# Threshold attention and a two-layer MLP on one core: the shared tile on the whole array, the last stores by halves, a reordered first pair, and the half-swapped k by GpSimd instead of DMA

## The chip, the cores and the metric

The kernel runs on one core of one Trainium2 chip. The metric is the device time of one execution in microseconds (us). Engine names in the profile: PE is TensorE, PEld its weight loads, DVE is VectorE, ACT is ScalarE, POOL is GpSimd, SP is the sync engine, and "SPq" is the sync engine's DMA issues.

## The reference

```python
# q, k, v: (8, 8, 576, 64), tau = 0.02
scores = q @ k.T / sqrt(64)
scores = where(scores >= max(scores) - tau, scores, -1e9)
attn   = exp(scores - max(scores)); attn /= sum(attn) + 1e-9
x      = (attn @ v)                  # heads side by side: (4608, 512)
h      = x @ w_in                    # 512 -> 2048
out    = (h - tanh(h)) @ w_out       # 2048 -> 512, (4608, 512) float32
```

## The kernel before

Heads are handled in pairs, 32 pairs in all, four pairs to a batch. A head has 576 = 4 x 128 + 64 queries, so a pair has nine tiles of 128 queries: four of each head, and the **shared tile** (number 4), which holds the 64 leftover queries of both heads. Each of q and k is split into an fp16 high and an fp16 low half, and TensorE transposes both into kT and qT (low and high stacked over the partitions). The cross terms need kS, which is kT with its two halves of 64 partitions swapped. While a batch's attention runs, the MLP of the batch before is woven in. The MLP weights are loaded in 16 pieces during the first seven pairs and cast by GpSimd, which also splits q and k.

Four parts matter. First, the way kS is made:

```python
m = qk_pool.tile([P, W], FP16, name=f"{t}T", tag=t)
nc.vector.tensor_copy(out=m, in_=ps)
...
sw = qk_pool.tile([P, W], FP16, name="kS", tag="ks")
nc.sync.dma_start(out=sw[0:D, :], in_=m[D:P, :])
nc.sync.dma_start(out=sw[D:P, :], in_=m[0:D, :])
```

Second, the shared tile in `attend`, and its two transposes in `emit_x`:

```python
for c in range(5):                       # shared tile: ten narrow products
    n = 64 if c == 4 else P
    for hh in range(2):
        nc.tensor.matmul(
            out=po[64 * hh : 64 * hh + 64, 4, :],
            lhsT=pt[0:n, c * P + 64 * hh : c * P + 64 * hh + 64],
            rhs=vb[0:n, hh, c, :], start=(c == 0), stop=(c == 4))
...
for hh in range(2):                      # and two 64x64 transposes
    s = slice(64 * hh, 64 * hh + 64)
    nc.tensor.matmul(out=ps[s, 512:576], lhsT=o[s, 4, 0, :],
                     rhs=ident_bf[s, s], is_transpose=True, ...)
```

Third, the stores of the last MLP block (the leftover rows of all batches, 128 rows at a time):

```python
rows = out.rearrange("(b s) n -> b s n", b=B)
to = rows[2 * ms : 2 * ms + 2, MB:S, :]          # (2, 64, 512)
stores.append(lambda: nc.sync.dma_start(out=to, in_=yo))
```

Fourth, the first pair: an activation table is loaded first, then k, q and v are loaded whole, split whole, and turned whole, and only then do scores start.

Of the kernel before, what the change touches and what calls it, by code (L numbers as in the profile page):

```python
# [9 lines left out]
F32 = mybir.dt.float32  # L10
# [8 lines left out]
def kernel(  # L19
# [12 lines left out]
    P = 128  # L32
# [58 lines left out]
    for i in range(NM):  # L91
        zm = const.tile([P, 5 * P], BF16, name=f"zm{i}")
        nc.vector.memset(zm[:, S : 5 * P], -STEEP)
        zms.append(zm)

    pool = lambda name, bufs, **kw: ctx.enter_context(
        tc.tile_pool(name=name, bufs=bufs, **kw)
    )
# [18 lines left out]
    ps_y = pool("ps_y", 1, space=PSUM)  # L117

    ctx.enter_context(tc.manual_schedule())
    warm = const.tile([P, 1], F32, name="warm")  # L120
    nc.vector.memset(warm, 0.0)
    nc.scalar.activation(out=warm, in_=warm, func=ACT.Exp)


    raws = {}
# [3 lines left out]
    def load(p, t):  # L129
        b, h0 = p // HPAIR, 2 * (p % HPAIR)  # L130
        hs = slice(h0, h0 + 2)
        src = {"k": k, "q": q, "v": v}[t]
        eng = nc.scalar if p == 0 and t == "q" else nc.sync
        r = raws[p, t] = raw_pool.tile([P, 10, D], F32, name=f"{t}raw", tag=t)
        n = 8 if t == "v" else 10
        eng.dma_start(
            out=r[:, 0:n, :].rearrange("p (h c) d -> p h (c d)", h=2)[:, :, 0 : 4 * D],
            in_=src[b, hs, 0:512, :].rearrange("h (p c) d -> p h (c d)", c=4),
        )
        if t == "v":  # L140
            rem = src[b, hs, 512:S, :].rearrange("h s d -> s h d")
            eng.dma_start(out=r[0:64, 8:10, :], in_=rem)
            eng.dma_start(out=r[64:P, 8:10, :], in_=rem)
        else:
            eng.dma_start(out=r[:, 4, :], in_=src[b, hs, 512:S, :])

    hls = {}

    def split(p, t, fast=False):
        r = raws.pop((p, t))[:, 0:9, :]  # L150
        hl = hl_pool.tile([P, TPP, 2, D], FP16, name=f"{t}hl", tag=t)
        if fast:
            nc.scalar.mul(out=hl[:, :, 0, :], in_=r, mul=QKSC)
            nc.vector.scalar_tensor_tensor(
                out=hl[:, :, 1, :], in0=r, scalar=QKSC, in1=hl[:, :, 0, :],
                op0=ALU.mult, op1=ALU.subtract,
            )
        else:
            x = hl_pool.tile([P, TPP, D], F32, name="xs", tag="xs")
            nc.gpsimd.tensor_scalar(  # L160
                out=x, in0=r, scalar1=QKSC, scalar2=1.0, op0=ALU.mult, op1=ALU.mult
            )
            nc.gpsimd.tensor_copy(out=hl[:, :, 0, :], in_=x)
            nc.gpsimd.tensor_tensor(  # L164
                out=hl[:, :, 1, :], in0=x, in1=hl[:, :, 0, :], op=ALU.subtract
            )
        hls[p, t] = hl

    def split_v(p):
        r, vb = raws.pop((p, "v")), vbs[p % NV]  # L170
# [8 lines left out]

    mats = {}  # L180

    def turn(p, t):
        hl = hls.pop((p, t))
        ps = ps_big.tile([P, W], FP16, name=f"ps_{t}", tag="big")
        for c in range(TPP):
            nc.tensor.matmul(  # L186
                out=ps[:, c * P : (c + 1) * P],
                lhsT=hl[:, c, :, :].rearrange("p a d -> p (a d)"),
                rhs=ident_f16, is_transpose=True, start=True, stop=True,
            )  # L190
        m = qk_pool.tile([P, W], FP16, name=f"{t}T", tag=t)
        nc.vector.tensor_copy(out=m, in_=ps)  # L192
        mats[p, t] = m
        if t == "k" and p == 0:
            ps = ps_big.tile([P, W], FP16, name="ps_ks", tag="big")
            for c in range(TPP):
                for a in range(2):
                    nc.tensor.matmul(
                        out=ps[64 * a : 64 * a + 64, c * P : (c + 1) * P],
                        lhsT=hl[:, c, 1 - a, :],  # L200
                        rhs=ident_f16, is_transpose=True, start=True, stop=True,
                    )
            sw = qk_pool.tile([P, W], FP16, name="kS", tag="ks")
            nc.vector.tensor_copy(out=sw, in_=ps)
            mats[p, "ks"] = sw
        elif t == "k":
            sw = qk_pool.tile([P, W], FP16, name="kS", tag="ks")
            nc.sync.dma_start(out=sw[0:D, :], in_=m[D:P, :])
            nc.sync.dma_start(out=sw[D:P, :], in_=m[0:D, :])
            mats[p, "ks"] = sw  # L210


    MAIN = (slice(0, 512), slice(640, W))
# [101 lines left out]
    def attend(i):  # L315

        p, j = divmod(i, TPP)
        kd, vb = kind(j), vbs[p % NV]
        if kd == "A":
            return  # L320
        if j in (1, 6):
            ops[p, int(j > 4)] = ps_o.tile([P, 5, D + 1], F32, name="psO", tag="o")
        po = ops[p, int(j > 4)]
        if kd == "M":
            pt = pts.pop(i)
            for c in range(5):
                n = 64 if c == 4 else P
                for hh in range(2):
                    nc.tensor.matmul(  # L329
                        out=po[64 * hh : 64 * hh + 64, 4, :],  # L330
                        lhsT=pt[0:n, c * P + 64 * hh : c * P + 64 * hh + 64],
                        rhs=vb[0:n, hh, c, :], start=(c == 0), stop=(c == 4),
                    )
            return
        pt, hh = pts.pop(i), int(j > 4)

        for ab in range(2):
            blocks = [(4 * ab + ab + c, c) for c in range(4)]
            blocks.append((4, 4 + ab))
            for n, (blk, c) in enumerate(blocks):  # L340
                nc.tensor.matmul(  # L341
                    out=po[:, (j - 1 - 5 * hh) + ab, :],
                    lhsT=pt[:, blk * P : (blk + 1) * P], rhs=vb[:, hh, c, :],
                    start=(n == 0), stop=(n == 4),
                )
# [3 lines left out]
    def norm(p, hh):  # L349
        po = ops.pop((p, hh))  # L350
        if hh == 0:
            osb[p] = o_pool.tile([P, 5, 2, D], BF16, name="osb")
        n = 5 - hh
        rc = st_pool.tile([P, 5], F32, name="rc", tag="rc")
        nc.vector.reciprocal(out=rc[:, 0:n], in_=po[:, 0:n, D])
        nc.vector.tensor_tensor(
            out=osb[p][:, 0:n, hh, :], in0=po[:, 0:n, 0:D],
            in1=rc[:, 0:n].unsqueeze(2).to_broadcast([P, n, D]), op=ALU.mult,
        )

    xs = {}

    def emit_x(p):
        o = osb.pop(p)
        ps = ps_h.tile([P, S], BF16, name="psX", tag="h")
        for t in range(4):
            nc.tensor.matmul(
                out=ps[:, t * P : (t + 1) * P],
                lhsT=o[:, t, :, :].rearrange("p a d -> p (a d)"),
                rhs=ident_bf, is_transpose=True, start=True, stop=True,  # L370
            )
        for hh in range(2):
            s = slice(64 * hh, 64 * hh + 64)
            nc.tensor.matmul(
                out=ps[s, 512:576], lhsT=o[s, 4, 0, :], rhs=ident_bf[s, s],
                is_transpose=True, start=True, stop=True,
            )
        b = p // HPAIR
        if p % HPAIR == 0:
            xs[b] = x_pool.tile([P, DM_C, MB], BF16, name="xT")  # L380
        nc.vector.tensor_copy(out=xs[b][:, p % HPAIR, :], in_=ps[:, 0:512])
        nc.vector.tensor_copy(out=xR[:, p % HPAIR, b, :], in_=ps[:, 512:S])


    gs, stores = {}, []
# [29 lines left out]
    def project(m, ms, part, ps, last):  # L415
        for n in range(4 * part, 4 * part + 4):
            nc.tensor.matmul(  # L417
                out=ps, lhsT=gs[m][:, n, ms * P : (ms + 1) * P],
                rhs=w_out_sb[:, n, :], start=(n == 0), stop=(n == DF_C - 1),
            )  # L420
        if part == 3:
            yo = y_pool.tile([P, d_model], F32, name="yo")
            if last:
                nc.scalar.copy(out=yo, in_=ps)
            else:
                nc.vector.tensor_copy(out=yo, in_=ps)  # L426
            if m < B:
                rows = out[m * S : m * S + MB, :].rearrange("(p c) n -> c p n", c=4)
                to = rows[ms]
            else:  # L430
                rows = out.rearrange("(b s) n -> b s n", b=B)
                to = rows[2 * ms : 2 * ms + 2, MB:S, :]
            stores.append(lambda: nc.sync.dma_start(out=to, in_=yo))

    def layers(m, tail):

# [66 lines left out]
        for d, f in PREP[3 if p == 1 else 0 :]:  # L503
            plan.setdefault(first - d, []).append(lambda p=p, f=f: f(p))

    for t in ("k", "q", "v"):
        load(0, t)
    for t in ("k", "q"):
        split(0, t, fast=True)
    for t in ("k", "q"):  # L510
        turn(0, t)
    split_v(0)
    for t in ("k", "q", "v"):
        load(1, t)
# [8 lines left out]
    for s in range(-AHEAD, NTILE + LAG + 3):  # L523
# [7 lines left out]
            shift(s + AHEAD - 1)  # L531
        if 0 <= s + AHEAD < NTILE:
            scores(s + AHEAD)
        if 0 <= s + MASK < NTILE:
            kink(s + MASK)
        bend()
# [79 lines left out]
```

## Time and profile before

| | before |
|---|---|
| median of 3 runs | 579.23 us (577.52 to 580.37) |
| span of the profiled run | 576.3 us |
| first score product starts | 12.33 us |
| pairs 1 to 4 together | 50.3 us |
| five batches, pairs 8 to 27 | 60.5, 60.7, 62.7, 60.7, 60.5 us |
| last TensorE product ends / tail after it | 561.6 us / 14.6 us |

A pair or batch is counted from the start of its first score product to that of the next one's, read from the TensorE records. A wait table gives engine, line, what it waited for: us in total, times, longest. The page's views are shown in the prediction and two more behind it; a wait table gives engine, line, what it waited for: us in total, times, longest. The first is the wait table of the sync engine's DMA queue (engine, line, what it waited for: us in total, times, longest):

```profile
SPq L208 <- DVE nb L257: 64.9, 27, 9.3
```

L208 is the first kS issue. The releaser is inferred from VectorE's semaphore, and nb is the small instruction beside it; in the timeline the kT copy on VectorE ends at 30.67 us and this issue starts at 30.70. So the sync engine, which issues nearly every load, the transposes of z and the stores in order, stands still at this line for 65 us of the run, 24.5 of them between 14 and 75 us. The second is GpSimd's wait table for 20 to 75 us:

```profile
POOL w_in_sb L473 <- DMA wt<-in_moe_w_in_dram: 15.4, 4, 6.3
```

GpSimd waits there for the weight loads that stand in that queue.

### The profile page before, as it was taken

Reading aid. Unit: us, or ns where it says so; the run is one execution under the profiler, and the core shown is the slowest. Engines: PE = TensorE matmul, PEld = TensorE weight load, DVE = VectorE, ACT = ScalarE, POOL = GpSimd, SP = SyncE. Lnnn points to the kernel's source line nnn. Section 1 sums busy time; section 2 is a strip of 40 time slices with the busy share of each in tenths; the row PEclk is TensorE's granted clock in tenths of the full one; section 3 lists DMA queues with packets and bytes.
Section 4 is the critical chain, followed back from the end, with each engine's and each line's share of the span. In section 5 each row is a group of like instructions: output and inputs, shape, how many; then the busy total and the mean of one; then the engine's idle time right before and its main releaser. Section 6 shows DMA issues by size and latency. Waiting matters only on the chain.

```text
span 576.3 us, 13882 instructions
## 1 busy us (share of the span) xinstructions
PE 535.3 (93%) x5146; PEld 303.6 (53%) x5146; DVE 442.6 (77%) x1312; ACT 440.1 (76%) x634; POOL 215.6 (37%) x310
## 2 busy tenths in 40 slices
PE   3889899999999999998999999999999999999990
PEld 2566566665555555554555555555555555444440
DVE  3888888888988988888888888888889896444410
ACT  1889898898888898887898988888889888333400
POOL 6646683753433344444444343345333400000000
PEclk9999999999999999999999999999999999999996
DMA  6556755448889999779989999998999865110111
GB/s 180 170 170 175 211 171 160 138 109 176 176 180 183 180 197 197 173 179 185 174 192 182 186 196 178 188 203 189 179 185 176 184 128 120 38 38 36 38 45 46
DMA packets 186923, 89.48 MB, mean 155 GB/s; under 512 B 150632, under 2 KB 175208, under 8 KB 186856
## 3 DMA queue, kind: packets, MB, share of 16 engines
q1 hardware_dynamic: 186454, 88.31, 70.2%
q8 instruction: 40, 0.66, 0.5%
q10 hardware_dynamic: 402, 0.29, 0.2%
q14 instruction: 27, 0.22, 0.1%
HBM read 37.75 MB, written 9.44 MB: 82 GB/s over the span
## 4 chain that ended last, share of the span: by engine, by line
PE 75%; DMA 6%; ACT 6%; DVE 6%; POOL 2%; issue 1%; SPq 1%; ACTq 0%; POOLq 0%; DVEq 0%
PE psY L417 20%; PE psH L391 17%; PE psS L242 17%; PE psO L341 5%; PE ps_k L186 3%; PE psS L232 3%; ACT pT L302 3%; DVE sc L248 3%; DMA kS<-kT 2%; PE psHt L391 2%; PE psZ L293 2%; ACT z L274 2%; PE psO L329 2%; PE ps_q L186 2%; DMA out_dram<-yo 2%
## 5 line engine op out<-in xcount | busy, mean ns | idle before, releaser
L248 DVE TENSOR_SCALAR_CACHE_REDUCE sc<-psS 128x576 f32<-128x576 f32 x288 | 216.4, 751 | 24.4 <-PE psS L232 10.8
L274 ACT ACTIVATE z<-sc,nb 128x576 bf16<-128x576 f32 x256 | 195.5, 768 | 27.2 <-DVE nb L257 26.0
L417 PE MATMUL psY<-w_out_sb,g 128*128 128x512 bf16 x576 | 145.4, 379 | 0.0
L310 ACT ACTIVATE pT<-zT 128x1152 f16<-128x1152 bf16 (+1 forms) x120 | 127.9, 1066 | 11.6 <-DMA zT<-z 11.0
L391 PE MATMUL psH<-xT,w_in_sb 128*128 128x512 bf16 x480 | 123.4, 379 | 0.0
L242 PE MATMUL psS<-kT,qT 128*128 128x512 f16 (+1 forms) x512 | 105.7, 288 | 8.4 <-DVE nb L257 4.7
L242 PEld LDWEIGHTS <-qT 128*128 128x128 f16 x1024 | 74.8, 98 | 70.7 <-issue 12.4
L242 PE MATMUL psS<-kS,qT 128*128 128x512 f16 (+1 forms) x512 | 105.8, 289 | 2.7 <-DMA kS<-kT 2.6
L410 DVE SCALAR_TENSOR_TENSOR g<-th,psH 128x512 bf16<-128x512 f32 x128 | 87.3, 682 | 25.3 <-ACT th L404 25.1
L404 ACT ACTIVATE th<-psH 128x512 f32<-128x512 f32 x128 | 74.5, 582 | 18.6 <-PE psH L391 18.4
L160 POOL TENSOR_SCALAR xs<-kraw 128x576 f32<-128x576 f32 x31 | 20.8, 669 | 165.9 <-DMA kraw<-in_k_dram 120.3
L417 PEld LDWEIGHTS <-g 128*128 128x128 bf16 x576 | 49.6, 98 | 57.7 <-issue 2.5
L391 PEld LDWEIGHTS <-w_in_sb 128*128 128x128 bf16 x576 | 48.9, 98 | 54.2 <-issue 2.7
L341 PEld LDWEIGHTS <-pT 128*128 128x128 f16 x1280 | 55.6, 98 | 24.3 <-ACT pT L310 2.1
L341 PE MATMUL psO<-vb,pT 128*128 128x65 bf16 x1280 | 61.2, 193 | 0.6 <-ACT pT L310 0.6
L302 ACT ACTIVATE pT<-psZ 128x640 f16<-128x640 bf16 (+1 forms) x72 | 47.1, 654 | 10.6 <-PE psZ L293 10.5
L257 DVE TENSOR_SCALAR nb<-mx 128x1 f32<-128x1 f32 x288 | 42.5, 147 | 3.4
L164 POOL TENSOR_TENSOR qhl<-xs,qhl 128x576 f16<-128x576 f32 x31 | 39.7, 1279 | 2.6
L164 POOL TENSOR_TENSOR khl<-xs,khl 128x576 f16<-128x576 f32 x31 | 39.6, 1279 | 2.7
L274 ACT ACTIVATE zm<-sc,nb 128x576 bf16<-128x576 f32 x32 | 24.7, 773 | 17.3 <-DVE nb L257 17.1
L192 DVE COPY qT<-ps_q 128x1152 f16<-128x1152 f16 x32 | 24.2, 755 | 11.5 <-PE ps_q L186 11.5
L426 DVE COPY yo<-psY 128x512 f32<-128x512 f32 x30 | 20.7, 689 | 13.7 <-DMA out_dram<-yo 8.0
(60 smaller groups left out, 505.5 us busy)
## 6 DMA issues: line engine op xcount, KB each, us to landing
out_dram<-yo SPq DMA_DIRECT2D x36, 256.0 KB
kS<-kT SPq DMA_DIRECT2D x62, 144.0 KB
kraw<-in_k_dram SPq DMA_DIRECT2D x32, 256.0 KB
vraw<-in_v_dram SPq DMA_DIRECT2D x32, 256.0 KB
qraw<-in_q_dram SPq DMA_DIRECT2D x31, 256.0 KB
wt<-in_moe_w_in_dram SPq DMA_DIRECT2D x8, 512.0 KB
wt<-in_moe_w_out_dram SPq DMA_DIRECT2D x8, 512.0 KB
vraw<-in_v_dram SPq DMA_DIRECT2D x64, 32.0 KB
```

Source lines behind the costliest of these rows:

```text
L164: nc.gpsimd.tensor_tensor(out=hl[:, :, 1, :], in0=x, in1=hl[:, :, 0, :], op=ALU.subtract)
L242: nc.tensor.matmul(out=ps[:, dst], lhsT=lhs, rhs=kk[:, src], start=(n == 0), stop=(n == 1),)
L248: nc.vector.tensor_scalar(out=sc, in0=ps[:, lo : lo + S], scalar1=SC, scalar2=None, op0=ALU.mult, op1=ALU.max, accum_out=mx,)
L257: nc.vector.tensor_scalar(out=nb, in0=mx, scalar1=-1.0, scalar2=tau, op0=ALU.mult, op1=ALU.add)
L274: nc.scalar.activation(out=z, in_=sc, func=ACT.Prelu, bias=nb, scale=1.0, alpha=STEEP)
L302: nc.scalar.activation(out=pt[:, off * P : (off + n) * P], in_=ps[:, 0 : n * P], func=ACT.Exp)
L310: nc.scalar.activation(out=pt[:, 0 : n * P], in_=zts.pop(i)[:, 0:n, :], func=ACT.Exp)
L341: nc.tensor.matmul(out=po[:, (j - 1 - 5 * hh) + ab, :], lhsT=pt[:, blk * P : (blk + 1) * P], rhs=vb[:, hh, c, :], start=(n == 0), stop=(n ...
L391: nc.tensor.matmul(out=ps, lhsT=w_in_sb[:, c, n * P : (n + 1) * P], rhs=xs[m][:, c, :] if m < B else xR[:, c, :, :], start=(c == 0), stop= ...
L404: nc.scalar.activation(out=th, in_=ps, func=ACT.Tanh)
L410: nc.vector.scalar_tensor_tensor(out=gs[m][:, n, :], in0=th, scalar=-1.0, in1=ps, op0=ALU.mult, op1=ALU.add,)
L417: nc.tensor.matmul(out=ps, lhsT=gs[m][:, n, ms * P : (ms + 1) * P], rhs=w_out_sb[:, n, :], start=(n == 0), stop=(n == DF_C - 1),)
```

## The change

The intent is to take narrow and mode-switching products off TensorE, to use all sixteen DMA engines for the last stores and for the first loads, to start scores sooner, and to take 62 transfers away from a nearly full DMA.

```diff
@@ k, half-swapped
-            nc.sync.dma_start(out=sw[0:D, :], in_=m[D:P, :])
-            nc.sync.dma_start(out=sw[D:P, :], in_=m[0:D, :])
+            nc.gpsimd.tensor_copy(out=sw[0:D, :], in_=m[D:P, :])
+            nc.gpsimd.tensor_copy(out=sw[D:P, :], in_=m[0:D, :])
@@ shared tile: both heads' columns at once, for all 128 queries
-                for hh in range(2):
-                    nc.tensor.matmul(out=po[64*hh : 64*hh+64, 4, :], ...)
+                nc.tensor.matmul(
+                    out=po[:, 4:6, :], lhsT=pt[:, c * P : (c + 1) * P],
+                    rhs=vb[:, :, c, :], start=(c == 0), stop=(c == 4))
@@ norm: `own` keeps for each query the head that it belongs to
+            nc.vector.scalar_tensor_tensor(
+                out=osb[p][:, 4, :, :], in0=po[:, 4:6, 0:D],
+                scalar=rc[:, 4:5], in1=own, op0=ALU.mult, op1=ALU.mult)
@@ emit_x: `fold` is the identity's two halves added
-        for hh in range(2): ... two 64x64 transposes
+        nc.tensor.matmul(out=pf[:, 256:320],
+            lhsT=o[:, 4, :, :].rearrange("p a d -> p (a d)"), rhs=fold, ...)
@@ last stores
-                to = rows[2 * ms : 2 * ms + 2, MB:S, :]
+                for h in range(2):       # 64 rows each
+                    stores.append(... out[b*S+MB : (b+1)*S, :] <- yo[64*h : 64*h+64, :])
@@ first pair
+    load_first("k", nc.sync)             # before the activation table,
+    load_first("q", nc.scalar)           # leftover rows as "h s d -> s h d"
+    ... split and turn chunks 0 to 4 first, chunks 5 to 8 in pair 0;
+    ... chunk 4, now interleaved, is transposed with every second identity column
```

(Cut: the leftover rows of all k and q loads are interleaved in the same way.)

## The prediction

> **What bounds the kernel now.** I read the page's busy table and slices first, then busy time by stage, then the timeline at two spots, the waits and the tail.
>
> ```profile
> PE 535.3 (93%) x5146; PEld 303.6 (53%) x5146; DVE 442.6 (77%) x1312; ACT 440.1 (76%) x634; POOL 215.6 (37%) x310
> PE   3889899999999999998999999999999999999990
> DMA  6556755448889999779989999998999865110111
> ```
> TensorE is busy in nearly every slice except the first and the last, and the DMA engines are almost full in the middle and almost idle in the last seven slices. The busy view by stage (window, length, then busy microseconds and count per engine, clock, DMA share, GB/s) cuts the run into three regimes:
>
> ```profile
> 24.00:74.00 50.00, 44.69 (x617) 31.57 (x616) 41.60 (x139) 45.19 (x74) 29.72 (x41) 1.00 0.66 191
> 178.50:239.20 60.70, 59.82 (x585) 33.42 (x584) 53.29 (x162) 52.50 (x73) 25.06 (x36) 1.00 0.95 184
> 482.00:562.00 80.00, 78.33 (x416) 36.21 (x412) 32.58 (x56) 29.43 (x47) 0.00 (x0) 1.00 0.14 45
> 562.00:576.30 14.30, 0.00 (x0) 0.00 (x0) 0.00 (x0) 0.58 (x1) 0.00 (x0) 0.65 0.12 46
> ```
> Before 74 us ScalarE leads (45.2 of 50) and TensorE has short waits. From about 74 to 482 us one batch takes some 60.7 us; TensorE is busy 59.8 of it, VectorE 53.3, ScalarE 52.5, and DMA sits at 95%: TensorE is the bound, DMA close behind. From 482 to 562 us TensorE works alone. The last 14.3 us hold one ScalarE instruction and 12% of DMA, which is two engines of sixteen: nothing but final stores. The head is a fourth regime: the first score product starts at 12.33 us.
>
> **What the Trainium skill says.** (1) "TensorEngine Tiling (Array Packing)", Key Properties: changing the tiling mode drains TensorE. The trace agrees, about 93 ns per switch (below). (2) "TensorE: Matmul & The Clock Gate", Back-to-back issue gap: N/2.4 + 2.5 ns. The trace agrees: N=512 products start 216 ns apart, N=128 ones 56 ns. (3) "DMA: Bandwidth & Descriptors", Why a DMA increments its semaphore by 16 and not by 1: a DMA uses the largest k up to 16 that divides the slowest dimension of both access patterns. A remainder store addressed as (2, 64, 512) gets k=2; the 12% share agrees. (4) "GPSIMD Engine Reference", Engine selection: one-input work is roughly line-rate. The casts agree: 662 ns for 576 elements, 1037 for 1024. No row here shows a copy across partitions.
>
> **The change part by part.**
>
> *Shared tile (64 leftover queries of each of two heads).* Now ten narrow products with two tiling modes, then two 64x64 transposes. Timeline:
>
> ```profile
> 308.05 1.04 PE L417 MATMUL psY<-w_out_sb,g 128*128 128x512 bf16 x4
> 309.01 0.47 PE L329 MATMUL psO<-vb,pT 128*64 128x65 bf16 x10
> 309.41 0.68 PE L186 MATMUL ps_k<-ident_f,khl 128*128 128x128 f16 x9
> ...
> 303.84 0.39 PE L367 MATMUL psX<-ident_bf,osb 128*128 128x128 bf16 x4
> 304.15 0.22 PE L374 MATMUL psX<-ident_bf,osb 64*64 64x64 bf16 x2
> 304.30 0.42 PE L242 MATMUL psS<-kT,qT 128*128 128x512 f16 x2
> ```
> Start to start, the block at L329 occupies 0.40 us. The four products before it take 0.96 instead of 4 x 0.216 = 0.86, so 0.09 is the switch in. Total 0.49. The change makes five full-array products with N=130: 5 x (130/2.4 + 2.5) = 0.28 us and no switch. Saved 0.21. At L374: 0.15 for the block, plus 0.31 - 4 x 0.056 = 0.09 of switch, 0.24; one N=64 product replaces it at about 0.03. Saved 0.21. Together 0.42 us per pair, 13.5 us over 32 pairs. Not all lies on the path: pairs 0 to 3 are paced by ScalarE, and in each batch's first pair there is a stretch without MLP products in which TensorE waits some 0.9 us for VectorE, where the L374 part is hidden. That leaves about 7 batches x (4 + 3) x 0.21 = 10 us. I take **-9**, as VectorE gains work: the 128x320 normalisation (491 ns) becomes 128x256 (424) plus one of 128 elements (about 290, by the line through 424 and 491): +0.22 us per pair, 0.9 in a batch. VectorE then stands at 54 of 59, still below.
>
> *Stores.* The last four are (2, 64, 512) and become eight of 64 rows.
>
> ```profile
> 546.78 14.84 PE L417 MATMUL psY<-w_out_sb,g 128*128 128x512 bf16 x68
> 560.00 0.69 DVE L426 COPY yo<-psY 128x512 f32<-128x512 f32 x1 [8.01 <-DMA out_dram<-yo]
> 565.09 0.58 ACT L424 COPY yo<-psY 128x512 f32<-128x512 f32 x1 [9.71 <-DMA out_dram<-yo]
> ```
> The last product ends at 561.62, but the last copy waits until 565.09 for a buffer that a slow store holds, and its own store then takes to 575.3. The 512 packets of 2 KB of these four stores run from 553.3 to 574.9 us: 5.4 us each, back to back on two engines. An ordinary 128-row store, 16 engines, runs its first packet 0.83 us after issue and its last at 1.66. After: 561.62 + 0.62 (copy and hand-over) + 0.35 (first half's issue) + 0.83 + 0.4 (half the packets) + 0.33 (landing) + 1.0 (end of program, as before) = 565.2 instead of 576.3. **-11**, entirely on the path.
>
> *First pair.* The k load's leftover rows are addressed (2, 64, 64) against 128 partitions, again two engines; k's split starts at 5.83. With leftover rows interleaved (64 outermost) all 16 serve, loads go out before the activation table is loaded, and only the first five chunks are split, transposed and copied before scores start. Walking it: data at about 3.7, split 0.45 + 0.5, five cold transposes 0.7, then q and swapped k, copies 0.5 each: first score near 7.3 instead of 12.33. The remaining four chunks come back in pair 0, where VectorE is 95% busy: about 1 us of split work. **-4**.
>
> *Swapped k.* 62 SBUF-to-SBUF DMAs go. TensorE waited for them:
>
> ```profile
> PEld L242 <- DMA kS<-kT: 4.2, 5, 2.2
> PE psS L242 <- DMA kS<-kT: 2.6, 3, 1.9
> ```
> The two rows are the same waits (loads and products of one sequencer). The product row is what delays: **-2.5**. It also removes the 512 packets of 2304 B per batch, 155 ns each, 512 x 155 / 16 = 5.0 us of 60: DMA falls from 95 to about 87%, which is what lets TensorE's gain arrive. In exchange GpSimd gets 62 copies 64x1152. Between 576 elements (662) and 1024 (1037) the slope is 0.84 ns, so 1152 take 1.15 us; 2.3 per pair, 71 us in all, on an engine at 215.6. In the steady stage: 25 + 9 = 34 of 60, hidden. The copies are placed five steps ahead of use, over 8 us, and need about 2.3 after kT. Before 74 us it is tight: per pair 5.2 (splits) + 1.2 (v) + 2.3 (weight casts at 2.25 x 1.04) + 2.3 = 11.0 of a 12.4 us period, in order behind weight loads. I charge **+2**.
>
> Sum: -9 - 11 - 4 - 2.5 + 2 = -24.5; 579.2 - 24.5 = **554.7 us**, -4.2%.
>
> **Rivals.**
> *GpSimd becomes the early bound.* For it: 11 of 12.4 us, and TensorE already waits once 1.05 us for khl at 66 us behind a 4.6 us weight load. Against: SP no longer stalls on the kS issues, so weights may come sooner. If a cross-partition copy costs twice the estimate, GpSimd needs 13.3 us per pair for six or seven pairs: +6 to +10, giving about 562. Steady state would still hide it.
> *VectorE, ScalarE or DMA takes over in the steady stage.* All stand near 88 to 90% with short look-ahead; then the shared-tile gain shrinks from 9 to 3 or so: 561. Against: TensorE's waits there are few and short.
> *Everything arrives.* Full 13 us on TensorE, 5 at the head, no early loss: 548.
> *Strided identity (every second column for chunk 4) streams slower.* 64 products; even 50 ns each is 3 us.
>
> **Range and chances.** The store part is nearly certain, and alone gives 568.2, just short of 2% faster (567.6). Head and shared tile have to fail together with a slow GpSimd to miss 2%. Range 547 to 563; faster 0.95, same 0.04, slower 0.01.
>
> **What would show it.** Right: no gap of 14 us after the last product, about 3.6 instead; first score near 7 us; no switch before the shared tile, about 0.28 us between its first product and the next group; batch near 59.2 us instead of 60.7; no wait of score products on kS; DMA near 0.87; kS copies near 1.15 us. Wrong: kS copies of 2 us or more, khl or kS waits on POOL in the first 75 us, batches still 60.7 us with new waits on VectorE or ScalarE results.

## The result, and the profile after

| | before | after |
|---|---|---|
| median of 4 runs of the same rounds | 578.87 us (577.52 to 580.37) | 551.54 us (551.16 to 551.85) |
| span of the profiled run | 576.3 | 549.4 |
| first score product | 12.33 | 7.99 |
| pair 0 | 10.2 | 11.6 |
| pairs 1 to 4 together | 50.3 | 48.4 |
| five batches | 60.5, 60.7, 62.7, 60.7, 60.5 | 59.3, 59.2, 59.2, 59.2, 59.2 |
| tail after the last product | 14.6 | 4.6 |

The ratio of after to before is 0.9527, with a 95% interval of 0.9502 to 0.9552: 4.7% faster. A ratio here is always the mean time of one kernel's fast runs over that of the other's fast runs of the same rounds, so it is not quite the ratio of the medians.

In the two profiled runs the difference of 26.9 us is spread as follows: 4.3 at the first score, of which pair 0 gives 1.4 back; 1.9 in pairs 1 to 4; 0.3 up to pair 8; 9.2 in the five batches (about 2 of that in one batch of 62.7 us in the trace before, in which TensorE waited 1.85 us for kS); 2.4 from pair 28 to the last product; 10.0 in the tail. The runs of the kernel after also lie closer together: 0.7 us from lowest to highest, against 2.9.

The page's busy row and DMA slices after (40 equal slices, each digit a busy share in tenths):

```profile
PE 521.8 (95%) x4954; PEld 302.4 (55%) x4954; DVE 444.1 (81%) x1349; ACT 443.3 (81%) x640; POOL 286.5 (52%) x372
...
DMA  6755644437879888889977798877878966310103
```

TensorE has 13.5 us less to do, GpSimd 71 us more, and the DMA is no longer full in the middle. The same by stage (window, length, busy us and count of PE, PEld, DVE, ACT, POOL, then clock, DMA share, GB/s):

```profile
20.00:70.00 50.00, 44.22 (x606) 32.07 (x605) 43.93 (x149) 47.36 (x76) 45.01 (x56) 1.00 0.56 170
170.00:229.00 59.00, 58.07 (x561) 33.40 (x560) 53.14 (x165) 52.60 (x73) 34.31 (x45) 1.00 0.84 170
540.00:549.40 9.40, 4.79 (x23) 1.96 (x20) 0.69 (x1) 0.59 (x1) 0.00 (x0) 0.92 0.33 77
```

In the first row ScalarE (47.4 of 50) leads, and GpSimd has come up to 45.0 (29.3 before). In the second, a whole batch takes 59 us, TensorE is busy 58.1 of it, and DMA stands at 84%.

The shared tile in the timeline of the kernel after (start, length, what):

```profile
296.32 1.04 PE L470 MATMUL psY<-w_out_sb,g 128*128 128x512 bf16 x4
297.19 0.45 PE L378 MATMUL psO<-vb,pT 128*128 128x130 bf16 x5
297.49 0.67 PE L221 MATMUL ps_k<-ident_f,khl 128*128 128x128 f16 x9
...
292.33 0.38 PE L421 MATMUL psX<-ident_bf,osb 128*128 128x128 bf16 x4
292.56 0.19 PE L427 MATMUL psX<-fold,osb 128*128 128x64 bf16 x1
292.58 0.41 PE L292 MATMUL psS<-kT,qT 128*128 128x512 f16 x2
```

The four products before the shared block now take 0.87 us from start to start instead of 0.96: the switch is gone. The block itself holds 0.30 us instead of 0.40. At the transposes, 0.25 us pass from the first of them to the next score, instead of 0.46.

The head and the tail:

```profile
5.96 0.71 PE L221 MATMUL ps_k<-ident_f,khl 128*128 128x128 f16 x5 [5.96 <-DVE khl L195]
6.47 0.73 PE L221 MATMUL ps_q<-ident_f,qhl 128*128 128x128 f16 x5
7.13 0.74 PE L221 MATMUL ps_ks<-ident_f,khl 128*64 128x128 f16 x10
7.99 0.66 PE L292 MATMUL psS<-kT,qT 128*128 128x512 f16 x2
...
541.37 0.69 DVE L479 COPY yo<-psY 128x512 f32<-128x512 f32 x1 [6.22 <-PE psY L470]
544.87 0.59 ACT L477 COPY yo<-psY 128x512 f32<-128x512 f32 x1 [6.32 <-PE psY L470]
```

The last two copies now wait for TensorE ("<-PE psY") and no longer for a slow store. And the cost of the new work on GpSimd and VectorE (groups of instructions: busy us, mean ns of one, and idle time before them):

```profile
L237 POOL COPY kS<-kT 64x1152 f16<-64x1152 f16 x31 | 35.3, 1140 | 141.4 <-DVE nb L307 141.4
L238 POOL COPY kS<-kT 64x1152 f16<-64x1152 f16 x31 | 35.4, 1142 | 1.3
L409 DVE SCALAR_TENSOR_TENSOR osb<-psO,rc,own 128x128 bf16<-128x128 f32 x32 | 10.9, 342 | 0.0
```

The 141.4 us are GpSimd standing idle until kT is there. That costs nothing on an engine that is busy for half the span, and only 2.7 us of it lie between 20 and 75 us, where it is short of time.

### The profile page after: what moved, and what is told of

Read it like the earlier page. It is cut to its first block, busy times and chain, and to the rows that moved or that the text cites. A ratio compares the mean times of both kernels' runs of the same rounds, so it can differ in the third digit from the quotient of the medians.

```text
span 549.4 us, 13518 instructions
## 1 busy us (share of the span) xinstructions
PE 521.8 (95%) x4954; PEld 302.4 (55%) x4954; DVE 444.1 (81%) x1349; ACT 443.3 (81%) x640; POOL 286.5 (52%) x372
## 4 chain that ended last, share of the span: by engine, by line
PE 72%; DVE 16%; ACT 8%; issue 2%; DMA 1%; SPq 0%; ACTq 0%; DVEq 0%
PE psY L470 20%; PE psH L444 18%; PE psS L292 15%; DVE sc L298 6%; PE psO L389 5%; ACT pT L352 4%; PE psS L282 3%; ACT z L324 3%; DVE g L463 3%; PE psHt L444 3%; PE ps_q L221 2%; PE ps_k L221 2%; PE psZ L343 2%; DVE yo L479 1%; DVE kT L233 1%
## 5 line engine op out<-in xcount | busy, mean ns | idle before, releaser
L237 POOL COPY kS<-kT 64x1152 f16<-64x1152 f16 x31 | 35.3, 1140 | 141.4 <-DVE nb L307 141.4
L292 PE MATMUL psS<-kS,qT 128*128 128x512 f16 x496 | 101.4, 286 | 0.0
L389 PE MATMUL psO<-vb,pT 128*128 128x65 bf16 x1280 | 61.2, 193 | 0.6 <-ACT pT L360 0.6
L352 ACT ACTIVATE pT<-psZ 128x640 f16<-128x640 bf16 (+1 forms) x72 | 47.2, 656 | 6.9 <-PE psZ L343 6.2
L238 POOL COPY kS<-kT 64x1152 f16<-64x1152 f16 x31 | 35.4, 1142 | 1.3
L343 PE MATMUL psZ<-ident_bf,z 128*128 128x128 bf16 x288 | 26.5, 219 | 4.5 <-ACT pT L352 4.3
```

The lines of the kernel that those rows point to most:

```text
L292: nc.tensor.matmul(out=ps[:, dst], lhsT=lhs, rhs=kk[:, src], start=(n == 0), stop=(n == 1),)
L352: nc.scalar.activation(out=pt[:, off * P : (off + n) * P], in_=ps[:, 0 : n * P], func=ACT.Exp)
L389: nc.tensor.matmul(out=po[:, (j - 1 - 5 * hh) + ab, :], lhsT=pt[:, blk * P : (blk + 1) * P], rhs=vb[:, hh, c, :], start=(n == 0), stop=(n ...
```

## The experiments

Twelve kernels ran, all with outputs that agree with the reference. The first four do one part of the change alone on the kernel before; five more change one thing of the kernel after, one more undoes a second part beside the first, and two try to go further. The medians of the kernel before in the rounds concerned were 578.42, 578.58 and 578.04 us. The kernel after was run in the first round only, against a median of 578.87, so a difference from it is good to about 1 us; where the ratios give another figure than the medians, both are said.

### The stores alone

```diff
 # kernel before
-                to = rows[2 * ms : 2 * ms + 2, MB:S, :]
+                for h in range(2): ... one store of 64 rows for each half
```

> The kernel before with only the eight 64-row stores in place of the four two-engine ones. Theory (the parts add, and the end of the program is nothing but stores on two engines): 10 us faster than before, about 568.8, with under 5 us between the last product and the end instead of 14.6; all else unchanged. Rival (the end is a fixed cost of landing and teardown): no more than 3 us faster.

Measured: 568.13 us (567.64 to 568.48), ratio 0.9827 (0.9810 to 0.9844), so 10.3 us less by the medians. The timeline of the tail:

```profile
552.55 11.40 SPq L434 DMA_DIRECT2D out_dram<-yo  x8
...
558.74 0.69 DVE L426 COPY yo<-psY 128x512 f32<-128x512 f32 x1 [6.21 <-PE psY L417]
562.24 0.59 ACT L424 COPY yo<-psY 128x512 f32<-128x512 f32 x1 [6.32 <-PE psY L417]
```

The last copy starts with the last product, and the tail is 4.5 us instead of 14.6. The batches stayed at 60.5 to 62.1 us. Two engines instead of sixteen were the cost of the old tail; the idea that the landing of a store has a fixed cost of this size falls.

### The shared tile alone

```diff
 # kernel before
+ five products of N=130, the mask, one folding product; kS still by DMA
```

> The kernel before with only the whole-array shared tile (five N=130 products, the mask, one folding product). Theory (TensorE is the bound from 74 to 482 us): 10 to 11 us faster, about 568, a batch 59.2 us instead of 60.7. Rival (another engine or the DMA at 95% takes over, and the swap by DMA has to go first): at most 5 us faster, batches at 60 us or more, new waits on the swapped k or on the transposes' DMA.

Measured: 573.33 us (571.55 to 573.75), ratio 0.9911 (0.9891 to 0.9931): 5.1 us, about half of what was expected. Two of the five batches reached the length of the kernel after (59.3 and 59.2 us), the others took 59.8 to 61.1. TensorE's waits in this run:

```profile
PE psS L251 <- DVE nb L266: 6.5, 12, 0.7
...
PE psS L251 <- DMA kS<-kT: 3.0, 4, 1.4
...
PE ps_k L195 <- POOL khl L173: 2.4, 2, 1.2
```

With less work between them, the products wait for kS (3.0 us) and for GpSimd's split (2.4, against 1.1 in the kernel before). So with kS still by DMA, the shared tile's gain arrives in part only.

### The swapped k alone

```diff
 # kernel before
-            nc.sync.dma_start(out=sw[0:D, :], in_=m[D:P, :])
-            nc.sync.dma_start(out=sw[D:P, :], in_=m[0:D, :])
+            nc.gpsimd.tensor_copy(out=sw[0:D, :], in_=m[D:P, :])
+            nc.gpsimd.tensor_copy(out=sw[D:P, :], in_=m[0:D, :])
```

> The kernel before with only the swapped k copied by GpSimd. Theory (TensorE waits 2 to 3 us for the swapped k, the rest of it is hidden): 2 to 3 us faster, about 576, DMA share in a batch near 0.86 instead of 0.95, no wait of products on the swapped k. Rival (GpSimd is tight before 74 us and costs what the waits gave): within 1 us of before, with pairs 1 to 4 longer than 12.6 us on average.

Measured: 573.41 us (572.78 to 574.03), ratio 0.9920 (0.9905 to 0.9934): 5.0 us less, about twice what was expected. All five batches took 60.5 us, so their jitter is gone; together they are 2.7 us shorter. Pairs 1 to 4 took 48.5 us instead of 50.3. That is the stage in which the prediction charged this part 2 us. By stage:

```profile
20.00:70.00 50.00, 45.41 (x623) 32.16 (x621) 43.09 (x142) 46.12 (x74) 45.20 (x55) 1.00 0.53 157
```

GpSimd went from 29 to 45.2 busy of 50 us, and yet TensorE did more in the window (45.4; the kernel before 44.1), not less.

### The first pair alone

```diff
 # kernel before
+ load_first, split_first, turn_first, and interleaved leftover rows
```

> The kernel before with only the new first pair and the interleaved leftover loads. Theory: the first score product starts near 8.0 us instead of 12.3, about 0.6 us is given back in the first pairs, so 3.5 to 4 us faster, about 575. Rival (the interleaved leftover loads on sixteen engines are worth as much, because they make every later DMA land sooner and end the waits on the swapped k): 6 us or more faster, with no wait of products on the swapped k.

Measured: 574.58 us (574.26 to 575.30), ratio 0.9943 (0.9923 to 0.9963): 3.8 us. The first score product started at 8.00 us, pair 0 took 11.4 instead of 10.2 us, and the batches stayed at 60.5 to 61.4. As expected. TensorE's waits on kS fell to 0.5 us (2.6 before), as the rival had it, but no gain went with that: pairs 1 to 4 took 51.0 us.

The four parts alone gain 10.3 + 5.1 + 5.0 + 3.8 = 24.2 us. Together they gain 27.3. Parts help each other, and the next runs ask which.

### The kernel after, with the swap back on the sync engine's DMA

```diff
 # kernel after
-            nc.gpsimd.tensor_copy(out=sw[0:D, :], in_=m[D:P, :])
-            nc.gpsimd.tensor_copy(out=sw[D:P, :], in_=m[0:D, :])
+            nc.sync.dma_start(out=sw[0:D, :], in_=m[D:P, :])
+            nc.sync.dma_start(out=sw[D:P, :], in_=m[0:D, :])
```

> The changed kernel with only the swapped k put back on DMA. Theory (the swap by GpSimd is worth the waits on the swapped k, 2 to 3 us): 553.5 to 554.5, products wait for the swapped k 2 to 3 us in all, DMA share 0.93 in a batch. Rival (with the leftover loads on sixteen engines the swapped k lands in time by DMA as well, and the GpSimd copies are worth nothing): within 0.7 us of the changed kernel, no such waits.

Measured: 560.14 us (559.50 to 564.41), ratio 0.9693 (0.9668 to 0.9718). As the last part to be added, the swap on GpSimd is worth 8.6 us by the medians and 9.6 by the ratios, more than either theory had. The sync engine's waits are back:

```profile
SPq L237 <- DVE nb L307: 54.2, 26, 8.1
```

and so are TensorE's waits for GpSimd's split (3.4 us before 74 us), although GpSimd has less to do than in the kernel after. The batches took 59.4 to 61.2 us instead of 59.2. The profiled execution was the slowest of the six, so its single stages are read with care.

### The same, with the leftover rows on two engines as before

```diff
 # the kernel of the last experiment
-            eng.dma_start(out=r[:, 4, :], in_=rem)
+            eng.dma_start(out=r[:, 4, :], in_=src[b, hs, 512:S, :])
```

> As the run before it, and with the leftover rows of q and k of pairs 1 to 31 loaded as before, on two engines. If the two-engine loads are what delayed the swapped k: 2 us or more slower than the run before it, and the waits on the swapped k are back. If the delay came from the queue of the transposes: the same as the run before it within 0.7 us.

Measured: 561.73 us (559.76 to 562.28), ratio 0.9704 (0.9684 to 0.9724): the same within the intervals. How the leftover rows are spread over engines is not why the DMA swap costs so much. This run's trace: pairs 1 to 4 took 51.3 us (after: 48.4), the batches 59.3 to 60.8. Of the 10.5 us that it is longer than the trace after, 2.9 lie in pairs 1 to 4, 5.0 in the five batches and 1.9 between pair 28 and the last product.

Where pairs 1 to 4 lose is to be seen in the start times of the weight loads and in the end of GpSimd's k splits. In this run weight loads six and seven went out at 45.2 and 45.8 us (in the kernel before at 46.6 and 47.2), together, right after a kS issue was released. In the kernel after they went out at 37.6 and 44.8. The fifth k split on GpSimd ended at 66.2 us (before: 67.3; after: 60.5), and pair 4, in which it falls, took 13.3 us (before 13.3; after 12.1).

### GpSimd's copies made twice

```diff
 # kernel after: the two copies are written a second time
+            nc.gpsimd.tensor_copy(out=sw[0:D, :], in_=m[D:P, :])
+            nc.gpsimd.tensor_copy(out=sw[D:P, :], in_=m[0:D, :])
```

> The changed kernel with each of the 62 GpSimd copies done twice (same result), 2.3 us more per pair. Theory (hidden after 74 us, tight before): GpSimd would need 13.3 us per pair against 12.1 to 12.3 us that a pair takes in pairs 1 to 4, so 4 to 6 us slower, all of it before 74 us; batches unchanged at 59.2 us. Rival (the lead of five steps hides it in the first pairs too): within 1 us.

Measured: 560.33 us (559.57 to 561.61), ratio 0.9686 (0.9665 to 0.9708), 8.8 us over the kernel after. Windows of the first stage and of a batch, and TensorE's first row of waits:

```profile
20.00:70.00 50.00, 40.90 (x539) 29.36 (x537) 39.10 (x131) 42.46 (x68) 47.12 (x57) 0.97 0.49 146
170.00:229.00 59.00, 58.12 (x561) 33.46 (x560) 53.14 (x165) 52.59 (x73) 43.46 (x53) 1.00 0.86 172
```
```profile
PE psS L294 <- POOL kS L240: 8.0, 8, 2.6
```

In the first stage GpSimd leads with 47.1 of 50 us, and pairs 1 to 5 took 12.6, 15.0, 12.6, 13.6 and 17.3 us, against 12.0 to 12.2 and 13.9 in the kernel after. That is 5.5 us in pairs 1 to 4, as the theory had it, and another 3.4 in pair 5, which ends at 91 us and which it had left out. In the later batches nothing changed: 59.2 us (the first took 59.5). So a second set of copies is more than the early stage holds, while one set is hidden, and later even two are.

### The kernel after, with the old transposes of the shared tile

```diff
 # kernel after
-        nc.tensor.matmul(out=pf[:, 256:320], lhsT=..., rhs=fold, ...)
+        for hh in range(2): ... two 64x64 transposes
```

> The changed kernel with the folding product of the shared tile put back to two 64x64 transposes; the five N=130 products stay. Theory (the tile switch and the small block cost 0.21 us per pair, and in one of four pairs that is hidden): 28 x 0.21 x 3/4 = 4.4 us slower than the changed kernel, a batch 0.63 to 0.65 us longer. Rival (it is the narrower second operand or VectorE's copy and not the switch): 1 us or less.

Measured: 556.52 us (556.27 to 556.92), ratio 0.9621 (0.9605 to 0.9636): 5.0 us more than the kernel after. Batches took 59.7 to 59.8 instead of 59.2 us, pairs 1 to 4 took 49.1 instead of 48.4, so the early pairs do not hide this cost altogether.

### The kernel after, with the whole old shared tile

```diff
 # kernel after: ten narrow products, one normalisation, two transposes again
```

> The changed kernel with the whole shared tile put back (ten narrow products, two small transposes, no mask); stores, first pair and GpSimd copies stay. Theory (the shared tile gave only 5 us by itself because the swapped k by DMA held it back; with GpSimd copies its whole 0.42 us per pair arrives in the batches): 9 to 10 us slower than the changed kernel, 561, every batch at 60.5 us. Rival (5 us is all that it is worth): 556 to 557.

Measured: 560.70 us (560.43 to 561.90), ratio 0.9704 (0.9689 to 0.9718): 9.2 us over the kernel after by the medians, 10 by the ratios. All five batches stood at 60.5 us. The shared tile gains 5.1 us with kS by DMA and 9 to 10 with kS by GpSimd (the two comparisons differ in the stores and the first pair as well, but those act at the two ends). This is where the parts help each other.

### The swap by DMA, issued by GpSimd

This was to separate two costs of the old way: that the sync engine stands still, and that a transfer has to be made at all.

```diff
 # kernel after
-            nc.gpsimd.tensor_copy(...)   # two
+            nc.gpsimd.dma_start(out=sw[0:D, :], in_=m[D:P, :])
+            nc.gpsimd.dma_start(out=sw[D:P, :], in_=m[0:D, :])
```

> The changed kernel with the swapped k moved by DMA again, but issued from GpSimd instead of the sync engine. Theory A (what cost 8.6 us was that the sync engine stood still at the swapped k's issue until kT was copied, and everything behind it in its queue came late): most comes back, 552 to 555, no waits of TensorE on khl before 74 us. Theory B (it is the transfer's own bytes and latency): as with the sync engine, 559 to 561, and products wait for the swapped k.

Measured: 575.11 us (570.94 to 577.28), ratio 0.9932 (0.9883 to 0.9982), worse than with the sync engine. The waits (TensorE), and the row of the DMA table (issuing engine, KB each, median us from issue to landing):

```profile
PE psS L292 <- DMA kS<-kT: 18.7, 13, 3.6
```
```profile
kS<-kT POOLq DMA_DIRECT2D x62, 144.0 KB, 3.8
```

The sync engine does not stand still for kS in this kernel, and TensorE does not wait for GpSimd's split any more. But the transfers landed 2.4 to 8.3 us after their issue, and TensorE waited 18.7 us for them; pair 1 took 15.1 us (after: 12.2), pairs 1 to 4 together 51.9, and two batches 63.9 and 68.4. So freeing the sync engine does not suffice where kS itself comes too late. With the sync engine (the swap put back) the last packet of kS had ended 2.1 to 3.9 us after the second of its two issues, so these transfers are slower, for a reason that no run tests, and the time of this run does not say how the 8.6 us divide between the two costs.

### Two attempts to go further

The first gives half of the mask transposes of the first batch another PSUM bank, and lets ScalarE issue every second half-store:

```diff
 # kernel after
-            ps = ps_y.tile([P, 5 * P], BF16, name="psZ", tag="y")
+            zp, zt_ = (ps_h, "h") if kd == "B" and i < HPAIR * TPP else (ps_y, "y")
+            ps = zp.tile([P, 5 * P], BF16, name="psZ", tag=zt_)
-                        lambda b=b, h=h: nc.sync.dma_start(
+                        lambda b=b, h=h: (nc.scalar if h else nc.sync).dma_start(
```

> The changed kernel with two edits that aim at what still waits: in the first batch the odd tiles' transposes go to the bank of the not yet used hidden layer, so that TensorE needn't wait for ScalarE to empty the only bank (3.7 us of waits in 12 places before 74 us), and the second half of the last stores is issued by ScalarE. If those waits are on the path: 1 to 2 us faster than the changed kernel, plus 0.5 at the end. If ScalarE (95% busy there) is the bound: 0.5 us, from the end alone.

Measured: 551.71 us (550.96 to 552.01), ratio 0.9542 (0.9528 to 0.9556): the same as the kernel after. The tail is 4.2 instead of 4.6 us. Before 74 us TensorE's waits for pT became fewer and longer (5.0 us in 6, instead of 3.7 in 12), while ScalarE stayed at 47.3 of 50. A second bank buys nothing where ScalarE is the limit.

The second also lets the masks of the second batch be transposed by DMA instead of TensorE:

```diff
 # the kernel of the last experiment
-    NPE = 2 * HPAIR * TPP
+    NPE = HPAIR * TPP
```

> As the run before it, and the second batch transposes its masks by DMA as the later ones do, which takes some 160 TensorE transposes out (36 tiles x 4.5 x 56 ns = 9 us) and gives ScalarE 75 ns less per tile. If TensorE or ScalarE bounds the second batch: 2 to 5 us faster than the run before it. If the transposes' DMA collides with the weight loads: no gain, or slower, with waits on zT.

Measured: 553.45 us (552.13 to 554.02), ratio 0.9571 (0.9556 to 0.9586), 1.7 us more. In the stage concerned, first this kernel, then the kernel after:

```profile
68.00:120.00 52.00, 41.43 (x405) 24.00 (x404) 42.30 (x135) 43.62 (x61) 37.97 (x46) 0.93 1.03 214
```
```profile
68.00:120.00 52.00, 49.56 (x595) 33.03 (x592) 45.05 (x144) 48.33 (x81) 37.97 (x46) 1.00 0.38 113
```

DMA went from 38% to full, and pairs 5 to 7 took 47.8 instead of 43.7 us. TensorE stands still for 10.6 us of the window instead of 2.4. No run beats the kernel after.

## Why the prediction was right

The total (24.5 us predicted, 27.3 measured by the medians) was right, and the range and the main mechanisms held. The difference lies almost wholly in one term. The parts can't simply be added: the shared tile and the swapped k depend on each other, and together they gave 13.2 us (27.3 less 10.3 for the stores and 3.8 for the first pair), where the sum had 9.5. The 8.6 and the 9 to 10 below, each measured as the last part, count a common piece of 4 to 5 us (by the medians) twice. The stores and the first pair fell 0.9 short together, so the small miss of the total (2.8 us) owes something to errors of opposite sign.

**Stores: 11 predicted, 10.0 to 10.3 measured.** The mechanism is shown by the run with the stores alone. The tail is 4.6 us instead of 3.6, because the packets of the last two half-stores ran for 1.40 us (140 ns each on average) where the prediction put 0.4, half of an ordinary store's 0.83 (86 ns each).

**First pair: 4 predicted, 3.8 measured.** The first score came at 7.99 rather than 7.3 us, and pair 0 gave back 1.4 rather than 1. The strided identity did no visible harm.

**Shared tile: 9 predicted, 9 to 10 measured, under the condition that the prediction named.** The timeline shows 0.40 of the 0.42 us per pair (0.09 + 0.10 at the products, 0.21 at the transposes) and the 59.2 us of a batch. The runs also bear out that the swap has to leave the DMA for the gain to arrive: alone, this part gains 5.1. That it is the lighter DMA, as the prediction had it, they do not show (see the swapped k). That ScalarE and short stretches would hide a part was too cautious, since putting the transposes back cost 5.0 us of a possible 6.7, and 0.7 of it in pairs 1 to 4. The mask took 342 ns instead of 290, and VectorE stands at 53.1 of 59 us, below TensorE, as predicted.

**Swapped k: 0.5 predicted (2.5 won, 2 charged), 5.0 alone and 8.6 as the last part measured.** This is the term that was mis-sized. The copies cost what was estimated (1.14 against 1.15 us), DMA in a batch fell to 84% (87 predicted), and TensorE's waits for kS vanished. By stages, the win came: with this part alone the five batches are 2.7 us shorter together, 2.2 of it in the one in which TensorE had waited 1.85 us for kS. The step that failed is the charge.

It was 2 us before 74 us, "in order behind weight loads". The sum of GpSimd's work was right: doubling the copies cost 8.8 us, in pairs 1 to 5. But one set fits, and pairs 1 to 4 got 1.8 us shorter (50.3 to 48.5 us with this part alone), since the weight loads on which GpSimd waited came sooner. The Trainium skill says why, on the page "DMA: Bandwidth & Descriptors", section Anatomy of one DMA: a DMA's semaphore wait is made on the issuing sequencer before the transfer is handed out. The trace agrees: the sync engine stood 64.9 us at the kS issue, waiting for kT, and every load behind it stood too. With the copies on GpSimd, its queue of loads waits for none of that; and from 20 to 75 us GpSimd's waits for weights went from 15.4 us to none. The sync engine now waits there for GpSimd to free a weight buffer. The prediction had this as a remark under its first rival ("SP no longer stalls on the kS issues, so weights may come sooner") and gave it no size.

That the swap is worth 8.6 us as the last part, and not 5.0, goes with a wait that stood on the page of the kernel before and that the prediction didn't read. The sync engine's queue also issues the DMA transposes that make zT, the input of ScalarE's exponentials from the third batch on. ScalarE's exponentials before, with the swap put back on DMA, and after (busy us, mean ns of one, then idle time before them):

```profile
L310 ACT ACTIVATE pT<-zT 128x1152 f16<-128x1152 bf16 (+1 forms) x120 | 127.9, 1066 | 11.6 <-DMA zT<-z 11.0
L360 ACT ACTIVATE pT<-zT 128x1152 f16<-128x1152 bf16 (+1 forms) x120 | 128.0, 1067 | 15.8 <-DMA zT<-z 15.6
L360 ACT ACTIVATE pT<-zT 128x1152 f16<-128x1152 bf16 (+1 forms) x120 | 127.8, 1065 | 0.0
```

From the end of z on ScalarE to the issue of its transpose 2.6 us pass on average in the kernel before, 2.8 with the swap put back, 0.8 in the kernel after. From issue to landing a transpose takes the same with the swap put back as after (median 3.4 and 3.3 us). So in the batches it is the standing queue, and not a fuller DMA, that delays zT; kS itself came in time there: with the swap put back the products wait for it once, 0.5 us, in pair 2. Between 120 and 420 us zT's transfers hold 8% of the chain that ended last with the swap put back (6% in the run with the leftover rows as before), and none of it after. This is read from the traces; no run moves the transposes alone to another queue, and how the 8.6 us divide over early pairs and batches is known from single traces only.

**Rivals.** "GpSimd becomes the early bound" came true only for copies of twice the cost, and then with 8.8 us, within the 6 to 10 that it gave. "VectorE, ScalarE or DMA takes over in the steady stage" did not happen in the kernel after. With the shared tile alone the gain did shrink, to 5.1; the trace shows TensorE waiting for kS and GpSimd's splits, and ScalarE 9.6 us for zT. "Everything arrives" (548) missed what came (551.5) by 3.5 us, the sum (554.7) by 3.2 on the other side.

## What to carry to other kernels

An issue that waits for a result can cost more than its transfer: it stops every later load and transpose of that queue, so before pricing a DMA that is to be removed read the queue's own waits, and the waits of the engines that are fed from behind it. Price the parts of a change against the kernel that will hold them all, since a part that shortens TensorE's work may arrive only once another part has removed the next wait. And for a store or load, look at the outermost dimension first: here an outermost dimension of 2 instead of 64 cost 10 us at the end of the kernel.

## What the Trainium skill lacked or had wrong

- "GPSIMD Engine Reference", section Cross-partition: it praises the engine for such moves, but has no figure for a plain copy from one half of the partitions to the other. Here a 64x1152 fp16 copy took 1.14 us, on the line through the straight casts (662 ns for 576 elements, 1037 for 1024).
- "TensorEngine Tiling (Array Packing)", section Tiling Modes, Key Properties: it says that a change of mode drains TensorE, but not what that costs. Here it cost about 0.09 us at each of two places per pair, and the products before the shared tile went from 0.96 to 0.87 us when it was gone.
- "DMA: Bandwidth & Descriptors", section Issuing engines are not separate DMA queues: it says that issuing from several engines only saves the time of the issue itself. Here the choice of issuer decided far more: an issue that waits held the sync engine's later loads and transposes for 64.9 us, and the kernel with the same swap took 560.1 us with the sync engine as issuer and 575.1 with GpSimd. The first-byte latencies in the page's Specifications, about 1 us for GpSimd and 0.6 for the sync engine, differ by 0.4 us and do not tell of the spread seen here: 2.4 to 8.3 us from issue to landing with GpSimd.
- "TensorE: Matmul & The Clock Gate", section Back-to-back issue gap: the formula that the prediction takes from it, N/2.4 + 2.5 ns, is there for the isolated gap; for a stream of weight loads and products in a real kernel the page gives about 81 ns at N=128 and 131 ns at N=512. In this kernel's streams the formula held instead: products of N=128 start 56 ns apart and those of N=512 216 ns.
